# An output product turned around: the stationary and the moving operand of the second MoE's last product change places, and the work beside it is spread differently

## The chip, the core and the metric

The kernel runs on one core of a Trainium2 chip, in one launch. The metric is the device time of that core in microseconds (us), as the median of the runs. A profiled execution gives the trace; its "span" is the time from the first to the last recorded event on the core, and its own run time is a little more than that.

## The reference, cut to what matters

Three parts follow one another: local attention over 4 x 8 heads x 768 positions (with 8 memory keys), a first MoE with a squared ReLU, and a second, gated MoE. All three run over the same 3072 tokens of width 512. The change touches only the end of the third part:

```
def _moe2_ref(x, w_gate, w_val, w_out):      # x: 3072 x 512
    g = x @ w_gate                           # 512 x 1536
    silu = g * (1.0 / (1.0 + np.exp(-g)))
    val = x @ w_val                          # 512 x 1536
    return (silu * val @ w_out)              # 1536 x 512  ->  3072 x 512
```

All is float32. The result is 3072 x 512.

## The kernel before, in words

**Precision.** Every float32 operand of a large product is split into a high part (a cast to fp32r, "hi") and the rest ("lo", the source minus hi). A product is three matmul passes: hi x hi, hi x lo, lo x hi. Making a split costs one cast on ScalarE (ACT, line 96) and one subtraction (line 99), on VectorE (DVE) or GpSimd (POOL), whichever the call names.

**Seven products for eight.** The second MoE treats its operands as 2 x 2 blocks and forms seven block products instead of eight, from sums of blocks. The sums of the weights are prepared earlier and lie in DRAM (`w2d`); the core streams them back four at a time, 1 MB (`load_chunks`, line 515), into five rotating buffers `wst`. The load of a group waits until the group five before it has been used.

**Stages.** The 3072 tokens are worked through in four stages s = 0 to 3 of 768 tokens (two halves of 384, `NT2`). A stage has two parts:

- The *gated* part (line 610), 12 blocks f of 7 products. A product (line 599) is six matmuls: the weight chunk is stationary (128 x 128), z, the stage's transposed input, moves 384 tokens wide. DVE and ACT combine the seven accumulators into two blocks of u = silu * val, which lie in `uf`, with tokens along the free dimension. Its accumulators are the four PSUM banks `abanks`.
- The *output* part (lines 844 to 856), called "b" in the plan: 42 items j, seven groups i of six (`NP`), one group for each block product of u with `w_out`. Here line 656 takes u as the stationary operand, 128 tokens at a time, and moves the weight sum 256 columns wide: three token tiles by three passes, nine matmuls for an item. A group adds up in one of two accumulators of two banks (`pbank`, line 581), used in turn. When a group is done, `combine` (line 681) reads that accumulator: ACT for group 0, DVE for the others (one instruction; two for group 5). The combination of group i is issued after item 6(i+1), and group i+2 may not begin before it has been read. Four of the seven combinations end in an output block of 384 tokens x 256 columns, which `store` (line 674) writes to DRAM from SyncE's queue, after the next item.

In the last stage the last group is taken apart instead: `item_rows` (line 663) forms one 128-token tile at a time over all six items, in a bank of its own, so that the combination (line 867) and the store of one tile run beside the next.

**The ring.** The items read hi and lo of a block of u from a ring of ten slots (`NRING`). Splits 0 to 9 are made in the gated part. The split for item j+10 is issued after item j, because it takes j's slot.

**Order.** All engines run in an order written out by hand; each engine works its own instructions strictly in that order. What runs beside the items is planned at lines 803 to 824: a dictionary from a place ("after item j") to the calls issued there. In the output part the plan holds, besides the 32 splits 10 to 41 (`split_u`; the subtraction on POOL where j % 3 == 2, else on DVE, line 816):

- the last block sums of u on POOL (`sum_u`): S1 and S2 of the last pair after item 0, and six S4, one after each of items 12 to 17 (line 814);
- in stages 0 to 2, the work on the next stage's z (lines 819 to 824): eleven calls at items 0 to 24: two splits of 128 x 768 (ACT cast, DVE subtraction), four block sums on DVE (line 563), and five more splits.

Within one place the order is: the combination, S4, the split of u, the work on z.

Of the kernel before, what the change touches and what calls it, by code (L numbers as in the profile page):

```python
# [7 lines left out]
F32 = mybir.dt.float32  # L8
# [4 lines left out]
ALU = mybir.AluOpType  # L13
# [11 lines left out]
DM, FF1, FF2 = 512, 2048, 1536  # L25
KD = DM // 128
NF1, NF2 = FF1 // 128, FF2 // 128
NTOK = B * S
BLOCKS = (4, 4, 4, 4, 4, 4, 4, 4)
NTM = GQ * max(BLOCKS)  # L30
NT2 = 384
# [13 lines left out]
QC = 2 * 128  # L45
NP = NF2 // 2
GVC, WOC = 7 * NF2, 7 * NP
NCH = GVC + WOC
NRING = 10
# [19 lines left out]
def attention_moe_moe_kernel(ctx, tc, att, v0, w1, w2, out):  # L69
# [8 lines left out]
    nc = tc.nc  # L78
    pe, act, dve, pool, sp = nc.tensor, nc.scalar, nc.vector, nc.gpsimd, nc.sync
# [9 lines left out]
    hbank = [ps.tile([128, 512], F32, name=f"hbank{i}") for i in range(2)]  # L89
    abank, yb0 = (ps.tile([128, 2, 512], F32, name=n) for n in ("abank", "yb0"))  # L90
# [24 lines left out]
    rows = []  # L115
# [195 lines left out]
    for t, n in enumerate(BLOCKS[1:], 1):  # L311
        for j in range(n):
            e = 13 * j + 12 if t == 1 else QB * (t - 1) + (j + 1) * QB // n - 15
# [201 lines left out]
    def load_chunks(g):  # L515
        if 4 * g >= NS * NCH:
            return
        t = chunks[g] = wp.tile([128, 4, 2, QC], R, tag="w", name="wst")
        n = 0
        while n < 4:  # L520
            c = (4 * g + n) % NCH
            m = min(4 - n, NCH - c)
            sp.dma_start(out=t[:, n:n + m].bitcast(F32), in_=w2d[:, c:c + m])
            n += m

    def chunk(n):
        t = chunks[n // 4]
        return [t[:, n % 4, h] for h in range(2)]
# [45 lines left out]
    def double():  # L574
        return up.tile([128, 2 * NT2], F32, tag="tmp", name="tmp", bufs=6)

    uf, ring = [], []
    SLOT = {"A11": 0, "A21": 1, "A12": 2, "A22": 3, "S3": 4, "S1": 1, "S2": 0, "S4": 2}
    ITEMS = ("A11", "A12", "S2", "S3", "A22", "S1", "S4")
    abanks = [*hbank, *yb1]  # L580
    pbank = [b.rearrange("p a c -> p (a c)")[:, 0:2 * NT2] for b in (abank, yb0)]

    def u_of(p, name):
        k = SLOT[name]
# [59 lines left out]
        dve.tensor_tensor(second, c22, u4, ALU.mult)  # L644
        side(6)

    def item(s, j):
        i, p = divmod(j, NP)
        uh, ul = ring[(WOC * s + j) % NRING]
        n = NCH * s + GVC + j  # L650
        whi, wlo = chunk(n)
        to = pbank[(7 * s + i) % 2]
        for t in range(3):
            rows = slice(128 * t, 128 * t + 128)
            for m, (u, wt) in enumerate(((uh, whi), (ul, whi), (uh, wlo))):
                pe.matmul(  # L656
                    to[:, QC * t:QC * t + QC], u[:, rows], wt,
                    start=p == 0 and m == 0 and t != 1, stop=p == NP - 1 and m == 2 and t != 0,
                )
        if n % 4 == 3:  # L660
            load_chunks(n // 4 + 5)

    def item_rows(s, t, to):
        rows = slice(128 * t, 128 * t + 128)
        for p in range(NP):
            j = 6 * NP + p
            uh, ul = ring[(WOC * s + j) % NRING]
            whi, wlo = chunk(NCH * s + GVC + j)
            for m, (u, wt) in enumerate(((uh, whi), (ul, whi), (uh, wlo))):
                pe.matmul(to, u[:, rows], wt, start=p == 0 and m == 0, stop=p == NP - 1 and m == 2)  # L670

    acc, ready = {}, []

    def store(s, h, e, o, t0=0, n=3):
        r0 = (2 * s + h) * NT2 + 128 * t0
        sp.dma_start(
            out=out[r0:r0 + 128 * n, e * QC:(e + 1) * QC].rearrange("(t p) c -> p t c", p=128),
            in_=o.rearrange("p (t c) -> p t c", c=QC),
        )

    def combine(s, i):
        p = pbank[(7 * s + i) % 2]
        if i == 0:
            acc["x"] = double()
            act.copy(acc["x"], p)
        elif i == 2:
            dve.tensor_tensor(acc["x"], p, acc["x"], ALU.add)  # L687
        elif i == 3:
            acc["y"] = double()
            dve.tensor_tensor(acc["y"], p, acc["x"], ALU.add)  # L690
        else:
            o = double()
            if i == 4:
                dve.tensor_tensor(o, acc["y"], p, ALU.subtract)
            else:
                dve.tensor_tensor(o, p, acc["y" if i == 5 else "x"], ALU.add)
            if i == 5:
                dve.tensor_tensor(acc["x"], p, acc["x"], ALU.add)
            h, e = {1: (0, 0), 4: (1, 0), 5: (1, 1), 6: (0, 1)}[i]
            ready.append((s, h, e, o))  # L700
# [19 lines left out]
    for c in range(NC2):  # L720
        a = QB * (P2 + c // 4) + (4, 18, 32, 44)[c % 4]
# [14 lines left out]
    def side(hs):  # L736
# [8 lines left out]
        out=eye, in_=eye, pattern=[[-1, GQ]], base=0, channel_multiplier=1, compare_op=ALU.is_equal, fill=0.0,  # L745
# [54 lines left out]
    def job(key, fn, *args):  # L800
        jobs.setdefault(key, []).append((fn, args))

    for s in range(NS):
        for p in range(NP):
            f = 2 * p + 1
            job((s, f, 0), split_u, s, p, pool)
            job((s, f, 1), sum_u, p, "S3")
            last_pair = p == NP - 1
            key = (s, "b", 0) if last_pair else (s, f + 1, 1)
            job(key, sum_u, p, "S1")  # L810
            job((s, "b", 0) if last_pair else (s, f + 1, 2), sum_u, p, "S2")
            if NP + p < NRING:
                job((s, f + 1, 4), split_u, s, NP + p, pool)
            job((s, "b", 2 * NP + p), sum_u, p, "S4")
        for j in range(NRING, WOC):
            job((s, "b", j - NRING), split_u, s, j, pool if j % 3 == 2 else dve)
        if s + 1 < NS:
            job((s, 6, 3), load_z, s + 1)
            for at_j, fn, *args in (
                (0, split_b1, 0), (2, split_b1, 1), (4, sum_t, "T1"), (6, sum_t, "T3"), (8, sum_t, "T2"),  # L820
                (10, sum_t, "T4"), (12, split_t, "T2"), (15, split_t, "T3"), (18, split_t, "T1"), (21, split_t, "T4"),
                (24, split_t, "B22"),
            ):
                job((s, "b", at_j), fn, s + 1, *args)

# [3 lines left out]
    for tags in (("gh", "gl"),) * 3 + (("r", "r"),):  # L829
        n = 3 if tags[0] == "gh" else 2  # L830
        ring.append([gp.tile([128, NTM], R, tag=tag, name="ring", bufs=n) for tag in tags])
    for _ in range(2):
        t = rawp.tile([128, WC], R, tag="cut", name="ring", bufs=CB)
# [6 lines left out]
    for s in range(NS):  # L840
        for f in range(NF2):
            gated(s, f, lambda slot: work(s, f, slot))
        final = s == NS - 1
        for j in range(WOC - NP * final):
            item(s, j)
            for args in ready:
                store(*args)
            ready.clear()
            if j and j % NP == 0:
                combine(s, j // NP - 1)  # L850
            work(s, "b", j)
        if not final:
            combine(s, 6)
            for args in ready:
                store(*args)
            ready.clear()
    s = NS - 1
    for t in range(3):
        p = abanks[t][:, 0:QC]
        item_rows(s, t, p)  # L860
        if t == 0:
            combine(s, 5)
            for args in ready:
                store(*args)
        cols = slice(QC * t, QC * t + QC)
        o = double()[:, 0:QC]
        dve.tensor_tensor(o, p, acc["x"][:, cols], ALU.add)
        store(s, 0, 1, o, t, 1)
    ordered.close()
    uctx.close()  # L870

# [67 lines left out]
```

## Time and profile before

| | |
|---|---|
| Time, median of 3 runs | 1152.96 us (1150.97 to 1153.2) |
| The profiled execution's own time | 1155.3 us |
| Its span | 1153.6 us, 22369 instructions |
| TensorE (PE) busy | 1137.2 us (99%), 8804 matmuls |
| VectorE (DVE) busy | 719.7 us (62%) |
| ScalarE (ACT) busy | 551.7 us (48%) |
| GpSimd (POOL) busy | 348.1 us (30%) |
| DMA | 245.24 MB, mean 213 GB/s |

"Busy" is the time in which an instruction of that engine was recorded as running. Matmuls are pipelined: one of 384 columns is recorded as 334 ns long, but the next one starts before it has ended. So PE's 99% does not say how many columns a microsecond carries; the step from one matmul to the next is read from the length of a run of matmuls in the chain of waits, divided by their number. A stage of the second MoE lasts about 134 us; the four output parts begin at 703, 837, 971 and 1105 us.

### The profile page before, as it was taken

What the parts mean: (1) busy time and instruction counts of PE and PEld (TensorE: products, weight loads), DVE (VectorE), ACT (ScalarE), POOL (GpSimd) and SP (SyncE); (2) the same over time, 40 slices, a digit from 0 to 9 for tenths busy, and PEclk for the clock granted to TensorE, in tenths of its full rate; (3) what the DMA queues carried; (4) which work ended last, traced back from release to release, by engine and by line L of the source; (5) the groups of instructions that cost most, each with busy time, mean ns of one, the idle gap of its engine ahead of it and who ended that gap; (6) DMA issues with size and microseconds to landing.
All of it is one profiled execution on the core that took longest, in us unless ns stands there. A gap on an engine that the chain in (4) does not pass through costs nothing.

```text
span 1153.6 us, 22369 instructions
## 1 busy us (share of the span) xinstructions
PE 1137.2 (99%) x8804; PEld 1120.9 (97%) x8804; DVE 719.7 (62%) x1216; ACT 551.7 (48%) x1348; POOL 348.1 (30%) x317
## 2 busy tenths in 40 slices
PE   6999999999999999999999999999999999999998
PEld 5999999999999999999999999999999999999998
DVE  6897445656655565563324668766696667956654
ACT  5896546666666667664452224322252223512242
POOL 0000001453425525250001335423371334713353
PEclk9999999999999999999999999999999999999999
DMA  9731204547665476550255866788777787787772
GB/s 376 298 126 53 89 27 152 205 169 254 213 216 193 172 238 245 197 178 9 83 182 236 290 219 214 260 276 293 270 265 262 259 309 252 243 292 254 255 283 98
DMA packets 81897, 245.24 MB, mean 213 GB/s; under 512 B 6272, under 2 KB 52864, under 8 KB 61568
## 3 DMA queue, kind: packets, MB, share of 16 engines
q1 hardware_dynamic: 81792, 243.82, 60.2%
q8 instruction: 69, 1.13, 0.4%
q14 instruction: 36, 0.29, 0.1%
HBM read 198.18 MB, written 45.61 MB: 211 GB/s over the span
## 4 chain that ended last, share of the span: by engine, by line
PE 96%; DVE 2%; DMA 1%; ACT 0%; issue 0%; SPq 0%; ACTq 0%; DVEq 0%
PE hbank L375 24%; PE yb L419 24%; PE hbank L605 15%; PE yb L605 15%; PE abank L656 7%; PE yb L656 6%; PE abank L272 2%; PE abank L150 2%; DVE ring L99 1%; PE hbank L210 1%; DMA first_v<-in_v_dram 1%; PE hbank L670 0%; DVE zraw L563 0%; DVE z L99 0%; DVE w L99 0%
## 5 line engine op out<-in xcount | busy, mean ns | idle before, releaser
L375 PE MATMUL hbank<-x,w 128*128 128x384 f32 (+1 forms) x1548 | 293.9, 338 | 0.0
L375 PEld LDWEIGHTS hbank<-x,w 128*128 128x128 f32 x1548 | 273.7, 191 | 0.8 <-issue 0.2
L400 DVE TENSOR_TENSOR gl<-r,gh 128x384 fp32r<-128x384 f32 x128 | 87.2, 682 | 228.7 <-ACT r L394 228.5
L419 PE MATMUL yb<-gh,w 128*128 128x384 f32 x1024 | 205.0, 337 | 0.0
L419 PEld LDWEIGHTS yb<-gh,w 128*128 128x128 f32 x1024 | 178.7, 188 | 2.2
L99 POOL TENSOR_TENSOR ring<-uf,ring 128x384 fp32r<-128x384 f32 x84 | 97.5, 1164 | 273.7 <-PE hbank L605 141.7
L592 POOL TENSOR_TENSOR uf<-uf 128x384 f32<-128x384 f32 x96 | 109.7, 1159 | 124.0 <-DVE uf L644 124.0
L605 PE MATMUL hbank<-w,wst 128*128 128x384 f32 x720 | 138.3, 334 | 0.0
L605 PE MATMUL yb<-w,wst 128*128 128x384 f32 x720 | 138.3, 334 | 0.0
L474 POOL TENSOR_TENSOR wraw<-cut 128x256 f32<-128x256 f32 x36 | 26.5, 737 | 347.1 <-DVE sm L239 262.8
L383 ACT ACTIVATE r<-hbank 128x384 f32<-128x384 f32 x128 | 63.0, 492 | 133.5 <-PE hbank L375 133.1
L605 PEld LDWEIGHTS hbank<-w,wst 128*128 128x128 f32 x720 | 126.0, 188 | 0.0
L605 PEld LDWEIGHTS yb<-w,wst 128*128 128x128 f32 x720 | 126.0, 188 | 0.0
L96 ACT CAST ring<-uf 128x384 fp32r<-128x384 f32 x168 | 85.9, 511 | 58.2 <-PE yb L656 28.9
L419 PE MATMUL yb<-gl,w 128*128 128x384 f32 x512 | 113.2, 334 | 0.0
L643 ACT ACTIVATE tmp<-tmp 128x384 f32<-128x384 f32 x48 | 25.2, 526 | 173.0 <-DVE tmp L642 173.0
L656 PE MATMUL abank<-wst,ring 128*128 128x256 f32 x756 | 93.1, 283 | 2.3 <-ACT ring L96 2.3
L656 PEld LDWEIGHTS abank<-wst,ring 128*128 128x128 f32 x756 | 91.8, 192 | 2.6 <-ACT ring L96 2.6
L419 PEld LDWEIGHTS yb<-gl,w 128*128 128x128 f32 x512 | 90.9, 188 | 0.0
L656 PE MATMUL yb<-wst,ring 128*128 128x256 f32 x702 | 86.4, 283 | 1.2 <-DVE tmp L687 1.2
L226 ACT ACTIVATE prob<-abank,mx 96x72 f32<-96x72 f32 x224 | 67.6, 310 | 40.6 <-DVE mx L218 40.3
L253 DVE STREAM_TRANSPOSE pT<-prob 32x256 f32<-32x256 f32 x196 | 85.1, 434 | 2.5
(128 smaller groups left out, 1513.6 us busy)
## 6 DMA issues: line engine op xcount, KB each, us to landing
wst<-w2d SPq DMA_DIRECT2D x124, 1024.0 KB, 5.0
wraw<-in_w_dram SPq DMA_DIRECT2D x34, 1024.0 KB, 6.4
qk<-in_att_dram SPq DMA_DIRECT2D x28, 464.0 KB, 5.3
w2d<-wraw SPq DMA_DIRECT2D x48, 256.0 KB, 2.5
v<-in_att_dram SPq DMA_DIRECT2D x28, 256.0 KB, 5.1
y1d<-ys SPq DMA_DIRECT2D x8, 768.0 KB, 4.5
w2d<-wraw SPq DMA_DIRECT2D x12, 512.0 KB, 3.0
zraw<-y1d SPq DMA_DIRECT2D x8, 768.0 KB, 7.9
```

The costliest lines, as they stand in the source:

```text
L96: act.copy(hi, src)
L99: lo_engine.tensor_tensor(lo, src, hi.bitcast(F32), ALU.subtract)
L226: act.activation(probs[u % 2][:, h, 0:WK], s["s"][:, r, i], AF.Exp, bias=s["mx"][:, r, i:i + 1], scale=SCALE, accum_out=s["sm"][:, h],)
L253: dve.transpose(pT[row:row + 32, :, 32 * c:32 * c + 32], probs[u % 2][32 * c:32 * c + 32, :, col:col + 32],)
L375: pe.matmul(hbank[f % 2][:, cols], wt[:, k * 128:(k + 1) * 128], x[:, k, cols], start=i == 0, stop=i == 3 * KD - 1,)
L383: act.activation(r, hbank[f % 2][:, 0:n], AF.Relu)
L400: dve.tensor_tensor(gl, g["r"], g["gh"].bitcast(F32), ALU.subtract)
L419: pe.matmul(ybank[e][:, 0:nt_of[t]], wt[:, c:c + 128], gtile[t, f][g], start=f == 0 and p == 0, stop=f == NF1 - 1 and p == 2,)
L474: pool.tensor_tensor(o, x, y, op)
L592: pool.tensor_tensor(u_of(p, o), u_of(p, x), u_of(p, y), op)
L605: pe.matmul(to, wt[:, k * 128:k * 128 + 128], x[:, k], start=m == 0, stop=m == 5)
L656: pe.matmul(to[:, QC * t:QC * t + QC], u[:, rows], wt, start=p == 0 and m == 0 and t != 1, stop=p == NP - 1 and m == 2 and t != 0,)
```

## The change

1. The output product is turned around. Line 656's matmul now has a 128-column slice of the weight sum as its stationary operand and moves u, 384 tokens wide; an item is two column halves k by three passes. The accumulator is one bank per half (128 output columns x 384 tokens, instead of 128 tokens x 256 columns by three). The output in DRAM becomes 512 x 3072, and is turned back outside the launch.
2. The combinations and the stores take the new layout (128 x 2 x 384 for 128 x 768; pieces of 384 elements in DRAM for pieces of 256).
3. The last group of the last stage is formed in two halves k instead of three token tiles.
4. The plan: S4 of pair p comes after item 5p + 4 (before: 12 + p). The subtraction of split j is on POOL where j % 4 == 1 (before: j % 3 == 2). The eleven calls on the next z stand after items 0, 3, 6, 9, 12, 15, 18, 22, 26, 30, 34 (before: 0, 2, 4, 6, 8, 10, 12, 15, 18, 21, 24), in the same order.

```diff
-    pbank = [b.rearrange("p a c -> p (a c)")[:, 0:2 * NT2] for b in (abank, yb0)]
+    pbank = [b[:, :, 0:NT2] for b in (abank, yb0)]
...
-    def item(s, j):
+    def item_pe(s, j, k, to):
         i, p = divmod(j, NP)
         uh, ul = ring[(WOC * s + j) % NRING]
+        whi, wlo = chunk(NCH * s + GVC + j)
+        for m, (u, wt) in enumerate(((uh, whi), (ul, whi), (uh, wlo))):
+            pe.matmul(
+                to[k], wt[:, 128 * k:128 * k + 128], u, start=p == 0 and m == 0, stop=p == NP - 1 and m == 2,
+            )
+
+    def item(s, j):
         n = NCH * s + GVC + j
-        whi, wlo = chunk(n)
-        to = pbank[(7 * s + i) % 2]
-        for t in range(3):
-            rows = slice(128 * t, 128 * t + 128)
-            for m, (u, wt) in enumerate(((uh, whi), (ul, whi), (uh, wlo))):
-                pe.matmul(
-                    to[:, QC * t:QC * t + QC], u[:, rows], wt,
-                    start=p == 0 and m == 0 and t != 1, stop=p == NP - 1 and m == 2 and t != 0,
-                )
+        to = pbank[(7 * s + j // NP) % 2]
+        for k in range(2):
+            item_pe(s, j, k, [to[:, 0], to[:, 1]])
...
-    def store(s, h, e, o, t0=0, n=3):
-        r0 = (2 * s + h) * NT2 + 128 * t0
+    def store(s, h, e, o, k0=0):
+        t0 = (2 * s + h) * NT2
+        n = o.shape[1]
+        r0 = e * QC + 128 * k0
         sp.dma_start(
-            out=out[r0:r0 + 128 * n, e * QC:(e + 1) * QC].rearrange("(t p) c -> p t c", p=128),
-            in_=o.rearrange("p (t c) -> p t c", c=QC),
+            out=out[r0:r0 + 128 * n, t0:t0 + NT2].rearrange("(k p) t -> p k t", p=128), in_=o,
         )
...
-            job((s, "b", 2 * NP + p), sum_u, p, "S4")
+            job((s, "b", 5 * p + 4), sum_u, p, "S4")
         for j in range(NRING, WOC):
-            job((s, "b", j - NRING), split_u, s, j, pool if j % 3 == 2 else dve)
+            job((s, "b", j - NRING), split_u, s, j, pool if j % 4 == 1 else dve)
...
-                (0, split_b1, 0), (2, split_b1, 1), (4, sum_t, "T1"), (6, sum_t, "T3"), (8, sum_t, "T2"),
-                (10, sum_t, "T4"), (12, split_t, "T2"), (15, split_t, "T3"), (18, split_t, "T1"), (21, split_t, "T4"),
-                (24, split_t, "B22"),
+                (0, split_b1, 0), (3, split_b1, 1), (6, sum_t, "T1"), (9, sum_t, "T3"), (12, sum_t, "T2"),
+                (15, sum_t, "T4"), (18, split_t, "T2"), (22, split_t, "T3"), (26, split_t, "T1"), (30, split_t, "T4"),
+                (34, split_t, "B22"),
...
     s = NS - 1
-    for t in range(3):
-        p = abanks[t][:, 0:QC]
-        item_rows(s, t, p)
-        if t == 0:
+    for k in range(2):
+        to = hbank[k][:, 0:NT2].rearrange("p (k n) -> p k n", k=1)
+        for p in range(NP):
+            item_pe(s, 6 * NP + p, k, [to[:, 0]] * 2)
+        if k == 0:
             combine(s, 5)
             for args in ready:
                 store(*args)
-        cols = slice(QC * t, QC * t + QC)
-        o = double()[:, 0:QC]
-        dve.tensor_tensor(o, p, acc["x"][:, cols], ALU.add)
-        store(s, 0, 1, o, t, 1)
+        o = double_k()[:, 0:1]
+        dve.tensor_tensor(o, to, acc["x"][:, k:k + 1], ALU.add)
+        store(s, 0, 1, o, k)
```

`double_k()` is `double()` (line 574) seen as 128 x 2 x 384.

## Rows read from the trace of the kernel before

**Rows 1.** The page, part 1 (busy time) and part 4 (chain's shares by engine):
```profile
PE 1137.2 (99%) x8804; PEld 1120.9 (97%) x8804; DVE 719.7 (62%) x1216; ACT 551.7 (48%) x1348; POOL 348.1 (30%) x317
PE 96%; DVE 2%; DMA 1%; ACT 0%; issue 0%; SPq 0%; ACTq 0%; DVEq 0%
```

**Rows 2.** The chain of waits over the span: start us, length us, work xmatmuls:
```profile
615.57 2.08 PE hbank L605 x12
...
702.93 6.47 PE abank L656 x54
...
722.36 6.49 PE yb L656 x54
729.95 6.71 PE abank L656 x54
...
749.62 2.08 PE hbank L605 x12
...
883.76 2.08 PE hbank L605 x12
...
971.13 6.47 PE abank L656 x54
...
1017.86 2.08 PE hbank L605 x12
...
1105.23 6.47 PE yb L656 x54
...
1144.10 4.32 PE hbank L670 x36
1148.41 2.17 PE yb L670 x18
```

**Rows 3.** Groups of PE instructions, whole span: count | busy us, mean ns | idle before:
```profile
L656 PE MATMUL abank<-wst,ring 128*128 128x256 f32 x756 | 93.1, 283 | 2.3 <-ACT ring L96 2.3
L656 PE MATMUL yb<-wst,ring 128*128 128x256 f32 x702 | 86.4, 283 | 1.2 <-DVE tmp L687 1.2
```

**Rows 4.** PE's timeline where stage 1's output part begins: start us, length us:
```profile
836.83 0.87 PE L656 MATMUL yb<-wst,ring 128*128 128x256 f32 x6
```

**Rows 5.** Who waited for whom, PE, 610 to 1154 us: total, times, longest:
```profile
PE abank L656 <- ACT ring L96: 2.3, 2, 1.2
PE yb L656 <- DVE tmp L687: 1.2, 1, 1.2
```

**Rows 6.** DVE's timeline in stage 0's output part: start us, length us, operation:
```profile
703.07 0.55 DVE L642 TENSOR_TENSOR tmp<-yb,tmp 128x384 f32<-128x384 f32 x1
...
704.75 0.55 DVE L99 TENSOR_TENSOR ring<-uf,ring 128x384 fp32r<-128x384 f32 x1
...
709.91 1.37 DVE L99 TENSOR_TENSOR ring<-uf,ring 128x384 fp32r<-128x384 f32 x1
711.20 0.95 DVE L563 TENSOR_TENSOR zraw<-zraw 128x768 f32<-128x768 f32 x1
...
721.65 1.77 DVE L99 TENSOR_TENSOR w<-tmp,w 128x768 fp32r<-128x768 f32 x1
...
725.92 1.77 DVE L99 TENSOR_TENSOR w<-zraw,w 128x768 fp32r<-128x768 f32 x1
...
728.90 0.94 DVE L687 TENSOR_TENSOR tmp<-abank,tmp 128x768 f32<-128x768 f32 x1
```

**Rows 7.** POOL's timeline in the same stretch:
```profile
721.24 4.35 POOL L592 TENSOR_TENSOR uf<-uf 128x384 f32<-128x384 f32 x3
...
739.51 1.01 POOL L99 TENSOR_TENSOR ring<-uf,ring 128x384 fp32r<-128x384 f32 x1 [2.20 <-ACT ring L96]
```

**Rows 8.** Stage 0's output part: length, busy of PE, PEld, DVE, ACT, POOL; clock, DMA:
```profile
702.77:749.62 46.85, 45.74 (x380) 45.56 (x380) 39.23 (x41) 21.89 (x41) 26.58 (x19) 1.00 0.75 250
```

**Rows 9.** The end, all engines' timeline:
```profile
1150.61 0.42 DVE L867 TENSOR_TENSOR tmp<-yb,tmp 128x256 f32<-128x256 f32 x1 [1.73 <-PE yb L670]
```

**Rows 10.** DMA issues from 1135 us to the end: count, KB each, median us to landing:
```profile
out_dram<-tmp SPq DMA_DIRECT2D x2, 384.0 KB, 2.6
out_dram<-tmp SPq DMA_DIRECT2D x3, 128.0 KB, 1.7
```

More of the change, by code (lines that the diff above doesn't have):

```diff
@@ L645, in gated, with double_k @@
         side(6)
-    def item(s, j):
+    def item_pe(s, j, k, to):
         i, p = divmod(j, NP)
         uh, ul = ring[(WOC * s + j) % NRING]
-        n = NCH * s + GVC + j
-        whi, wlo = chunk(n)
-        to = pbank[(7 * s + i) % 2]
-        for t in range(3):
-            rows = slice(128 * t, 128 * t + 128)
-            for m, (u, wt) in enumerate(((uh, whi), (ul, whi), (uh, wlo))):
-                pe.matmul(
-                    to[:, QC * t:QC * t + QC], u[:, rows], wt,
-                    start=p == 0 and m == 0 and t != 1, stop=p == NP - 1 and m == 2 and t != 0,
-                )
+        whi, wlo = chunk(NCH * s + GVC + j)
[4 more added lines that the diff above has]
+    def item(s, j):
+        n = NCH * s + GVC + j
+        to = pbank[(7 * s + j // NP) % 2]
+        for k in range(2):
+            item_pe(s, j, k, [to[:, 0], to[:, 1]])
         if n % 4 == 3:
             load_chunks(n // 4 + 5)
[L663 to L670, printed above, removed]
-    acc, ready = {}, []
-    def store(s, h, e, o, t0=0, n=3):
-        r0 = (2 * s + h) * NT2 + 128 * t0
+    acc, ready = {}, []
+    def double_k():
+        return double().rearrange("p (k n) -> p k n", k=2)
+    def store(s, h, e, o, k0=0):
+        t0 = (2 * s + h) * NT2
+        n = o.shape[1]
+        r0 = e * QC + 128 * k0
         sp.dma_start(
-            out=out[r0:r0 + 128 * n, e * QC:(e + 1) * QC].rearrange("(t p) c -> p t c", p=128),
-            in_=o.rearrange("p (t c) -> p t c", c=QC),
+            out=out[r0:r0 + 128 * n, t0:t0 + NT2].rearrange("(k p) t -> p k t", p=128), in_=o,
         )
@@ L683, in combine @@
         if i == 0:
-            acc["x"] = double()
+            acc["x"] = double_k()
             act.copy(acc["x"], p)
@@ L688, in combine @@
         elif i == 3:
-            acc["y"] = double()
+            acc["y"] = double_k()
             dve.tensor_tensor(acc["y"], p, acc["x"], ALU.add)
         else:
-            o = double()
+            o = double_k()
             if i == 4:
@@ L933 @@
         args.append(nc.dram_tensor(f"in_{name}_dram", a.shape, _mybir.dt.from_np(a.dtype), kind="ExternalInput").ap())
-    args.append(nc.dram_tensor("out_0_dram", (NTOK, DM), F32, kind="ExternalOutput").ap())
+    args.append(nc.dram_tensor("out_0_dram", (DM, NTOK), F32, kind="ExternalOutput").ap())
     with _tile.TileContext(nc) as tc:
@@ L937 @@
     r = _run(nc, [arrays], core_ids=[0])
-    return r.results[0]["out_0_dram"]
+    return _np.ascontiguousarray(r.results[0]["out_0_dram"].T)
```

## The prediction

> **What bounds the kernel now.** I read the page first. PE is busy 99% of the span and makes up 96% of the chain that ended last [rows 1]; no other engine carries more than 2% of it. So the time moves when PE's stream gets shorter or when PE stops waiting inside it, and hardly otherwise. Busy time doesn't tell how long the stream is, because matmuls overlap. For that I went to the chain of waits, which prints runs of matmuls with a start and a length [rows 2]. Two steps come out of it:
>
> - the 384-wide matmuls with a weight chunk stationary (line 605): 2.08 us for 12, that is 173.3 ns from one to the next;
> - the 256-wide matmuls of the output part (line 656): 6.48 us for the 54 of a group (6.47 and 6.49 are printed), that is 120.0 ns.
>
> The stage table gives a granted clock of 1.00 in the output part [rows 8], full speed, 2.4 GHz: 384 columns are 160.0 ns there and 256 are 106.7 ns. Both steps stand 13.3 ns above their columns. A matmul thus costs its columns plus the same 13.3 ns here, whatever its width.
>
> Second, the waits inside the stream. An output part of 42 items without a wait lasts 7 x 6.48 = 45.36 us. From the starts in the chain [rows 2], stage 0 takes 749.62 - 702.93 = 46.69 us, stage 2 takes 1017.86 - 971.13 = 46.73. For stage 1 the chain leaves PE at the start, so I take it from PE's timeline, which shows matmuls 0.16 us ahead of the chain's reckoning (702.77 opens the stretch of rows 8, 702.93 the chain's run): 836.83 + 0.16 = 836.99 [rows 4], so 883.76 - 836.99 = 46.77. Lost: 1.33 + 1.41 + 1.37 = 4.11 us. Stage 3, which has no next z to prepare, takes 1144.10 - 1105.23 = 38.87 for six groups, 6 x 6.48 = 38.88: nothing lost.
>
> Where is it lost? In stage 0 the fourth group ends at 722.36 + 6.49 = 728.85 and the fifth begins at 729.95, 1.10 us late, and then runs 0.23 us longer (6.71). The table of waits has one such wait per stage, 2.3 and 1.2 us in all, two of them put down to ACT's cast into the ring and one to DVE's line 687 [rows 5]. The first name misleads. Group 4 uses the accumulator of group 2, and line 687 is what empties it; DVE ran it at 728.90 for 0.94 us [rows 6], just up to the late start, although group 2 had ended at 722.36. DVE was some 6.5 us behind. So PE waits once per z stage for DVE's backlog.
>
> **The change part by part.** *The matmuls.* An item goes from 9 x 120.0 = 1080 ns to 6 matmuls of 384. The columns stay the same (2304); three matmuls go, with 3 x 13.3 = 40 ns. The trace of before has no item of the new form. From both sides: line 605 with the same width and the same kind of stationary tile (`wst`) gives 173.3 ns, 1040 ns an item; if the step of line 656 grew with its columns, it would be 180.0 ns and nothing would be gained. I take 173.3, as the nearest row in width, operand and clock. Count: line 656 has 756 + 702 = 1458 matmuls [rows 3], line 670 has 36 + 18 [rows 2]: 1512, or 168 items. 1512 x 120.0 = 181.4 us become 1008 x 173.3 = 174.7: **-6.7 us** (0 to -6.7).
>
> The Trainium skill ("TensorE: Matmul & The Clock Gate", section "Back-to-back issue gap") gives N / 2.4 + 2.5 ns for a warm matmul, and by that rule turning the product around is worth next to nothing: 3 x 2.5 = 7.5 ns an item, an estimated 1.3 us in all. The rows don't follow it: both widths stand 13.3 ns above their columns, not 2.5. It is a rival below for the case that the new form comes nearer to it.
>
> *The wait for DVE.* Line 687 of group 2 is issued after item 18; group 4 begins with item 24. Items get shorter, so PE is there earlier: 24 x 1.040 = 24.96 us after the start of the part, instead of 25.92. What stands ahead of line 687 on DVE, from the plan:
>
> - before: the subtractions of splits 10 to 27 less the six on POOL, 12; four z subtractions (places 0, 2, 12, 15); four z sums; one combination;
> - after: 14 subtractions (four on POOL); two z subtractions (0, 3; the others are at 18 and later, behind line 687); four sums; one combination.
>
> DVE's operations on two SBUF operands come in two lengths: 0.55 or 1.37 us for 384 columns, 0.95 or 1.77 for 768 [rows 6]. The difference, 0.82 us, is the same at both, and it goes with POOL running: POOL's own operation takes 4.35 / 3 = 1.45 us beside DVE and 1.01 alone [rows 7]. So a POOL operation costs DVE up to 0.82 us. POOL has 14 ahead of that point before (S1, S2, six splits, six S4) and 9 after (S1, S2, four splits, S4 of items 4, 9, 14). The sum for DVE, from its start on this queue 1.82 us into the part (704.75 - 702.93):
>
> - before: 12 x 0.55 + 4 x 0.95 + 4 x 0.95 + 0.95 = 15.2; 14 x 0.82 = 11.5; with 0.94 for line 687 itself and 1.82: 29.4 us. Measured: 729.84 - 702.93 = 26.9. The sum is 2.5 too high, since not every POOL operation meets one of DVE's.
> - after: 14 x 0.55 + 2 x 0.95 + 4 x 0.95 + 0.95 = 14.4; 9 x 0.82 = 7.4; with 0.94 and 1.82: 24.5 us at most.
>
> 24.5 is before 24.96 even with every meeting counted; with the surplus of the sum before taken off in proportion (2.5 x 9 / 14 = 1.6) it is 22.9, and the accumulator is free 2 us early. The wait is gone: **-4.1 us** over three stages. From both sides: if all that DVE gained were the two z subtractions (2 x 1.77) less two more splits at their worst (2 x 1.37), line 687 would end 0.8 us earlier, with PE 0.96 earlier too: the late start would be 1.10 + 0.96 - 0.80 = 1.26, with the 0.23 after it 1.49 a stage, 4.5 in all, 0.4 more than now. Below nothing isn't to be had.
>
> *What is late next.* The second half gets what the first half loses. A POOL operation cost DVE (11.5 - 2.5) / 14 = 0.64 us on average before; I use that from 22.9 us on. Line 690 (group 3) has to end before item 30, at 31.2 us: ahead of it stand four subtractions of u, two of z and three POOL operations, with its own 0.94 together 6.9 us, so it ends near 29.8. Line 694 (group 4) has to end before item 36, at 37.4: five of u, one of z, three of POOL and 0.94 are 6.5, so near 36.3. Both hold, with 1.1 to 1.4 us in hand. The last z split is issued after item 34 (36.4 us); its result (B22) is first read by the seventh product of the next gated part, 43.7 + 6 x 1.04 = 49.9 us after the start. The splits of u have a lead of nine items (9.4 us), and DVE is at most some 4 us behind (22.9 less 18.7, where item 18 begins). POOL's 19 operations become 16; S4 of pair 5 comes after item 29, its split after item 31, ten items before item 41. Nothing of POOL is late.
>
> *What costs nothing.* Combinations read the same 768 columns. SyncE's queue holds the stores ahead of chunk loads, and a store waits for its combination; DVE comes earlier, so the loads behind it aren't later. Chunks are needed every 4.16 us instead of 4.32, the pace of the gated part (4 x 6 x 173.3 ns), in which PE waited for nothing [rows 5]. All of this is hidden by PE's stream; the bare price would show as PE waiting for `wst`.
>
> *The end.* The last group is in the 168 items. Behind the last matmul stands one DVE operation of 384 columns, 0.55 [rows 6], for one of 256, 0.42 [rows 9]; and a store of 192 KB for 128 KB. 384 KB landed in 2.6 us and 128 in 1.7 [rows 10], so 192 is near 1.9: **+0.35 us** (0 to +1.0).
>
> *Sum.* -6.7 - 4.1 + 0.35 = -10.5 us. The profiled execution (span 1153.6, 1155.3 in all, 1.7 outside) would become a span of 1143.1 and 1144.8; it lies 2.3 above the median of the runs. Against the median: 1152.96 - 10.5 = **1142.5 us**. Where no item waits, z stages' output parts last 42 x 1.040 = 43.7 us.
>
> **The rivals.**
>
> 1. *The wait stays, or moves to a later group.* PE arrives 0.96 us earlier and DVE gains no more than that, or line 690 or 694 is late in place of line 687. For it: the lower bound above, and margins of only 1 us in the second half. Against it: five POOL operations fewer ahead of line 687. Then 1152.96 - 6.7 + 0.4 + 0.35 = 1147.0; half of it, 1144.8.
> 2. *The new form saves less.* By columns alone, 180.0 ns a matmul, it saves nothing: 1152.96 - 4.1 + 0.35 = 1149.2. Against it: line 605's 173.3 ns at that width. By the Trainium skill's rule above, 2.5 ns for each of 504 matmuls fewer, it would be an estimated 1147.9.
> 3. *Slower: DVE becomes the bound of the z stages.* It now has 24 of the 32 subtractions of u instead of 21. If each of its 35 operations on two SBUF operands met POOL: 24 x 1.37 + 11 x 1.77 + 7 x 0.94 = 58.9 us against 43.7. Its last z result is read 6.2 us into the next part, so the output part would last about 58.9 - 6.2 = 52.7 us, 6 longer than now, and the kernel 1152.96 + 3 x 6 - 1.3 (stage 3 and the end) = 1169.7. It begins to decide when DVE takes more than 43.7 + 6.2 = 49.9 us. Against it: POOL has only 16 operations, at most 16 x 0.82 = 13.1 us of meetings on 24 x 0.55 + 11 x 0.95 + 7 x 0.94 = 30.2, that is 43.3; DVE is busy 39.2 us in the same stretch now [rows 8].
>
> **How the numbers follow.** The forecast has 0.78 (1141 to 1144.2: the runs shown spread by 1 us either side, and the end is open by some tenths); the wait that stays in whole or half or moves, 0.13 (1144.8 to 1147); the new form saving less, 0.05; slower by DVE, 0.02; the rest is for what I don't see. The range 1140.8 to 1147.0 holds the first two cases. 0.2%, 2.3 us, is about what a measurement of this kernel can tell from no change: faster by more 0.95, within 0.03, slower 0.02.
>
> **What would show it.** In the profile after, the items' matmuls run in the chain at 6.24 us for 36, 173.3 ns each; 6.48 us for 36 would be by columns. The three z stages' output parts last 43.7 us and the stage-3 one 6 x 6.24 = 37.4; line 687's combination of group 2 ends before item 24, and PE's table of waits has no entry in them. If it still has one at the fifth group, the step on DVE's queue is wrong; if it has one at another group, the step on the second half is. A new wait for `wst` or a part beyond 47 us would make the whole wrong.

## The result

| | before | after |
|---|---|---|
| Time, median | 1152.93 us (1150.97 to 1153.2, 4 runs) | 1142.83 us (1140.31 to 1143.89, 4 runs) |
| Ratio to before | | 0.9913, 95% interval 0.9893 to 0.9932 |
| Span of the profiled execution | 1153.6 us | 1141.0 us |
| Matmuls | 8804 | 8300 |

Forecast was 1142.5 us. The page after, its busy times and its chain by engine:

```profile
PE 1128.5 (99%) x8300; PEld 1112.5 (98%) x8300; DVE 717.4 (63%) x1227; ACT 551.8 (48%) x1348; POOL 328.1 (29%) x305
PE 98%; DMA 1%; SPq 0%; DVE 0%; ACT 0%; issue 0%; ACTq 0%
```

DVE's 2% of the chain [rows 1] is gone, and PE's table of waits has no entry between 600 us and the end. The chain of waits after (start us, length us, work; the items are line 652 now):

```profile
700.85 6.24 PE abank L652 x36
707.09 6.24 PE yb L652 x36
713.33 6.24 PE abank L652 x36
719.57 6.24 PE yb L652 x36
725.81 6.24 PE abank L652 x36
732.05 6.24 PE yb L652 x36
738.29 6.24 PE abank L652 x36
...
831.89 6.24 PE yb L652 x36
...
869.33 6.24 PE yb L652 x36
...
962.93 6.24 PE abank L652 x36
...
1000.37 6.24 PE abank L652 x36
...
1093.97 6.24 PE yb L652 x36
...
1125.17 6.24 PE abank L652 x36
1131.41 6.26 PE hbank L652 x36
```

Each group begins where the one before it ends. The output part of stage 0 takes 744.53 - 700.85 = 43.68 us, and so do those of stages 1 and 2 (875.57 - 831.89, 1006.61 - 962.93), for 46.69, 46.77 and 46.73 before [rows 2, 4]. A matmul takes 6.24 / 36 = 173.3 ns.

DVE's timeline in stage 0, its line for group 2's combination being 683 now, then those for groups 3 and 4:

```profile
722.70 0.94 DVE L683 TENSOR_TENSOR tmp<-abank,tmp 128x768 f32<-128x768 f32 x1
...
727.17 0.94 DVE L686 TENSOR_TENSOR tmp<-yb,tmp 128x768 f32<-128x768 f32 x1
...
733.72 0.94 DVE L690 TENSOR_TENSOR tmp<-tmp,abank 128x768 f32<-128x768 f32 x1
```

Group 2's ends at 723.64, 22.8 us into the part (26.9 before [rows 6]); item 24 begins at 725.81. The stage's row (length, busy of PE, PEld, DVE, ACT, POOL, clock, DMA), against [rows 8]:

```profile
700.69:744.53 43.84, 43.84 (x254) 43.84 (x254) 37.51 (x44) 22.01 (x41) 21.28 (x16) 1.00 0.78 270
```

DVE executes three operations more than before and is busy 1.7 us less, beside three operations fewer on POOL (e6 to e8 below bear on that).

The two profiled spans differ by 12.6 us, not by 10.5. From the start of stage 0's output part to the last matmul's end (702.93 to 1150.58 before, 700.85 to 1137.67 after) the kernel lost 10.83 us: 6.72 + 4.11 as summed up. The end grew from 3.02 to 3.33. The other 2.08 us were gone before stage 0's output part began, in code that is the same in both: 0.69 us had been gained when a run of 40 matmuls near 32 us began, right after the opening's loads, and 1.42 us in this run (0.03 came back behind it), whose length differs between executions. In the chains of before, after, and e1 below:

```profile
31.92 10.39 PE hbank L375 x40
```
```profile
31.23 8.97 PE hbank L375 x40
```
```profile
30.96 7.03 PE hbank L375 x40
```

That is 260, 224 and 176 ns a matmul of 288 columns, where 120.0 ns of columns and 13.3 would be 133 (an estimate from the two steps of the prediction). The table of stretches gives the granted clock as 1.00 over this run, in before too (third number from the end):

```profile
31.92:42.31 10.39, 10.39 (x41) 10.39 (x42) 6.68 (x11) 6.15 (x23) 0.00 (x0) 1.00 1.02 418
```

So the trace does not show what holds PE there, and the cause stays open. The run took 6.67 to 10.39 us in the eleven profiles that have it whole. The two shortest belong to e1 and e5, in executions some 3 us faster than the median of their kernels, so this run may be most of the 3 us by which runs of one kernel differ; an execution without a trace can't show it.

### The profile page after: what moved, and what is told of

The parts are those of the page before. It is cut to its first block, busy times and chain, and to the rows that moved or that the text cites. A ratio compares the mean times of both kernels' runs of the same rounds, so it can differ in the third digit from the quotient of the medians.

```text
span 1141.0 us, 21345 instructions
## 1 busy us (share of the span) xinstructions
PE 1128.5 (99%) x8300; PEld 1112.5 (98%) x8300; DVE 717.4 (63%) x1227; ACT 551.8 (48%) x1348; POOL 328.1 (29%) x305
## 4 chain that ended last, share of the span: by engine, by line
PE 98%; DMA 1%; SPq 0%; DVE 0%; ACT 0%; issue 0%; ACTq 0%
PE hbank L375 24%; PE yb L419 24%; PE yb L605 15%; PE hbank L605 15%; PE abank L652 8%; PE yb L652 7%; PE abank L272 2%; PE abank L150 2%; PE hbank L210 1%; DMA first_v<-in_v_dram 1%; PE hbank L652 1%; PE yb L192 0%; SPq L125 0%; DVE x L287 0%; DVE tmp L863 0%
## 5 line engine op out<-in xcount | busy, mean ns | idle before, releaser
L99 POOL TENSOR_TENSOR ring<-uf,ring 128x384 fp32r<-128x384 f32 x72 | 81.1, 1126 | 283.5 <-ACT ring L96 143.7
L592 POOL TENSOR_TENSOR uf<-uf 128x384 f32<-128x384 f32 x96 | 106.1, 1116 | 123.6 <-DVE uf L644 123.6
L652 PE MATMUL abank<-ring,wst 128*128 128x384 f32 x504 | 89.6, 334 | 0.0
L652 PEld LDWEIGHTS abank<-ring,wst 128*128 128x128 f32 x504 | 87.6, 188 | 0.0
L652 PE MATMUL yb<-ring,wst 128*128 128x384 f32 x468 | 83.2, 334 | 0.0
```

Of the source, the lines that this page charges most:

```text
L99: lo_engine.tensor_tensor(lo, src, hi.bitcast(F32), ALU.subtract)
L592: pool.tensor_tensor(u_of(p, o), u_of(p, x), u_of(p, y), op)
L652: pe.matmul(to[k], wt[:, 128 * k:128 * k + 128], u, start=p == 0 and m == 0, stop=p == NP - 1 and m == 2,)
```

## The experiments

Theory: the turned product saves 40 ns an item, and DVE's backlog, which the plan removes, keeps an accumulator occupied. Rivals: the wait was for ACT's cast into the ring; or the new product, not the plan, removed it; or another law for the step of a matmul.

**e1: the product alone**, with the old plan.

```diff
-            job((s, "b", 5 * p + 4), sum_u, p, "S4")
+            job((s, "b", 2 * NP + p), sum_u, p, "S4")
-            ... pool if j % 4 == 1 else dve)      # z at 0, 3, 6, ... 34
+            ... pool if j % 3 == 2 else dve)      # z at 0, 2, 4, ... 24
```

> The product turned around (384 wide, six matmuls an item), with the old plan for the next z, S4 and the subtractions. Theory (DVE's backlog holds the accumulator, and only the plan removes that): group 2's combination ends 26 to 27 us after the start of a z stage's output part, as before, while item 24 could now begin at 24.96; so PE waits once per z stage, at the fifth group, 1.5 to 2.2 us, longer than the 1.1 us before, with 0.2 us after it. Output parts of the z stages 45.4 to 46.1 us, stage 3 without a wait; 1142.8 + 3 x 2.1 = about 1149. Rival (the new layout of the accumulators, one bank per column half, by itself lets DVE empty them in time): no wait, output parts 43.7 us, 1142.8.

1154.63 us (1151.21 to 1155.29, 10 runs), ratio to before 1.001 (0.9997 to 1.0024): the turned product alone gains nothing, and the time is 5.6 us above the theory's forecast. The chain gives the output parts as 46.8, 48.4 and 46.8 us, 10.9 us of waits and their sequels in all. Three things are in its rows.

```profile
717.93 6.52 PE yb L652 x36
726.46 6.48 PE abank L652 x36
...
860.63 8.07 PE yb L652 x36
```

DVE's rows for the accumulators of groups 1 and 2:

```profile
716.84 0.94 DVE L692 TENSOR_TENSOR tmp<-yb,tmp 128x768 f32<-128x768 f32 x1
...
725.41 0.94 DVE L683 TENSOR_TENSOR tmp<-abank,tmp 128x768 f32<-128x768 f32 x1
```

First, group 3 starts late too (717.93 for 717.36): it needs group 1's accumulator, and line 692 empties that only at 717.78. I had looked at group 4 only. Second, group 4 begins 2.02 us after group 3's end and 2.86 us after the place that it could have had (698.64 + 24.96 = 723.60), where 1.5 to 2.2 were expected: group 2's combination ends at 726.35, 27.7 us into the part, and not 26 to 27. Group 3's late start adds nothing to this, because group 4 waits for that combination in any case. The group behind each wait takes 0.24 to 0.28 us more; with group 4's 0.24 a stage loses 3.1 us. Third, in stage 1 group 4 takes 8.07 us for 6.24. The stage table of that stretch (columns as above; the third from the end is the granted clock):

```profile
860.00:862.00 2.00, 1.36 (x8) 1.40 (x9) 2.00 (x4) 0.05 (x1) 0.47 (x1) 1.00 0.29 119
862.00:864.00 2.00, 2.00 (x8) 2.00 (x7) 2.00 (x4) 1.58 (x3) 0.00 (x0) 0.52 0.00 0
864.00:866.00 2.00, 2.00 (x9) 2.00 (x9) 2.00 (x4) 0.54 (x2) 1.01 (x1) 0.62 0.68 164
866.00:868.00 2.00, 2.00 (x13) 2.00 (x12) 1.53 (x3) 0.92 (x3) 0.00 (x0) 1.00 0.85 360
```

After a wait of 2.13 us the granted clock fell to half and stayed there over most of 4 us: another 1.6 us. In this profile the waits of about 2.0 us in stages 0 and 2 had no such sequel. Of the waits of before, none over 1.2 us, none had one. Averaged over the span, the granted clock was 0.997 to 0.999 in the ten runs of e1 and 1.000 in the fifteen of before. That fits such falls in more than the one profile, but the runs without a trace do not show where the clock was lower.

**e2: the plan alone**, with the old product.

> The old product (256 wide, nine matmuls an item) with the new plan for the next z, S4 and the subtractions. Theory: the wait goes with the plan alone, each output part is 42 x 1.080 = 45.36 us, and the kernel gains 4.1 us: 1148.8. Rival (the wait went because of the new product): the wait of 1.1 + 0.23 us stays in each z stage, 1152.9.

1149.25 us (1146.83 to 1150.03, 6 runs), ratio 0.9957 (0.9943 to 0.9972). Every group takes 6.48 us and follows the one before; PE's table of waits has no entry in these parts. The fourth and fifth groups of stage 0 in the chain:

```profile
720.74 6.48 PE yb L656 x54
727.22 6.48 PE abank L656 x54
```

As the theory has it, the plan removes the wait by itself. Together with e1: the plan alone is worth 3.9 us, the product alone -1.5 (before beside them: 1153.13), both 10.1 (before beside it: 1152.93). The two parts are not independent.

**e4 and e4b: a third accumulator** under the old plan, so that DVE may stay late.

> As e1_product_only (new product, old plan), but the groups use three accumulators in turn instead of two (the third one in the two banks that the gated part leaves free); the last group of the last stage goes to the two other free banks. Theory (PE waits for DVE to empty the accumulator of group 2, not for ACT's cast into the ring): the fifth group now needs the accumulator of group 1, long empty, and the wait goes though DVE is as late as in e1 (group 2's combination still ends 25 to 27 us into the part): output parts 43.7 us, 1142.8. Rival (the wait is one for ACT's cast into the ring, as the table of waits calls it): the wait at the fifth group stays, 1149.

1247.69 us (4 runs), ratio 1.0814 (1.0792 to 1.0835). I had made one tile of the two banks `hbank`, and in the gated part PE now waited wherever DVE or ACT still read the other bank of that tile. The largest of seven such entries (line 606 is the product, 636 a sum):

```profile
PE hboth L606 <- DVE tmp L636: 13.4, 12, 1.1
```

The gated part of stage 1 grew from 87.4 to about 109 us. So the total says nothing on the question; the output parts took 43.7 us without a wait. e4b repeats it with the banks as two tiles:

```diff
+        i = j // NP
+        to = [b[:, 0:NT2] for b in hbank] if i % 3 == 2 else [pbank[i % 3][:, 0], pbank[i % 3][:, 1]]
...                                          # combinations of groups 2 and 5: one instruction for each bank
-        to = hbank[k][:, 0:NT2].rearrange("p (k n) -> p k n", k=1)
+        to = yb1[k][:, 0:NT2].rearrange("p (k n) -> p k n", k=1)
```

> New product, old plan, three accumulators in turn as in e4_third_accumulator, but the third one stays two separate one-bank tiles (hbank), so that the gated part is untouched; the combinations of groups 2 and 5 are two instructions of 384 columns each instead of one of 768. Theory (PE waits for DVE to empty an accumulator, and nothing else in these parts is late): every wait of e1 goes, output parts 43.7 us in all stages, 1142.8, though the plan is the old one and the combination of group 2 still ends 25 us or more after the start. Rival (DVE's lateness also holds the ring or SyncE's queue of chunk loads, so that it costs in any case): waits stay, at later items, and the time lies between 1146 and 1155.

1143.17 us (1140.26 to 1143.63, 4 runs), ratio 0.9911 (0.9894 to 0.9927), the changed kernel's time with the old plan. The chain, then DVE's row for group 2:

```profile
720.28 6.24 PE abank L652 x36
726.52 6.24 PE yb L652 x36
```
```profile
728.33 1.01 DVE L687 TENSOR_TENSOR tmp<-hbank,tmp 128x384 f32<-128x384 f32 x2
```

DVE is as late as in e1 (729.34, 27.8 us into the part), and the fifth group starts at 726.52 all the same. So in e1 PE waited for an occupied accumulator and for nothing else in these parts. The two entries that named ACT's cast [rows 5] were the same wait under another name.

**e5, e6, e7: one part of the plan back**, in the changed kernel.

> The changed kernel with only the work on the next z at its old places (0 to 24). Ahead of group 2's combination stand 14 subtractions of u, four of z, four sums, one combination and nine POOL operations at 0.64 to 0.82 us: it ends 24.8 to 26.4 us into the part, against 24.96 for item 24. Theory: a wait of 0 to 1.4 us at the fifth group in each z stage, without the fall of the clock that came after 2.0 us: 1143 to 1148, about 1146. Rival (the places of z carry the whole gain of the plan): as e1, 1154.6. Rival (z is not what made DVE late): 1142.8.

> The changed kernel with only the six S4 back at items 12 to 17. DVE's own work ahead of group 2's combination is that of the changed kernel, but 12 POOL operations instead of 9 stand beside it: 24.8 to 27.0 us at 0.64 to 0.82 us each, against 24.96. Theory (POOL's operations on two SBUF operands hold DVE's up): a wait of 0 to 2 us at the fifth group of the z stages, 1143 to 1149, about 1145.5. Rival (POOL's sums don't matter to DVE): 1142.8.

> The changed kernel with only the old choice of POOL's subtractions (j % 3 == 2: 11 of 32, instead of 8). Ahead of group 2's combination: 12 subtractions of u on DVE instead of 14, 11 POOL operations instead of 9: 23.1 to 25.1 us against 24.96. Theory: two subtractions fewer on DVE (1.1 us) are outweighed by two more meetings with POOL (1.3 to 1.6), but the margin holds in most groups: 1142.8 to 1144. Rival (giving DVE more subtractions made it later, so that the old choice leaves more room): 1142.8 with the combination of group 2 ending earlier than in the changed kernel (723.64 - 700.85 = 22.8 us).

| put back | median us (range) | ratio to before (95%) | z stages' output parts, us | late groups |
|---|---|---|---|---|
| e5: places of z | 1145.15 (1142.52 to 1146.41) | 0.993 (0.9913 to 0.9947) | 44.41, 44.49, 44.48 | 3 and 4 |
| e6: S4 | 1143.93 (1141.47 to 1144.2) | 0.9918 (0.9903 to 0.9932) | 44.01, 44.03, 44.02 | 4 |
| e7: choice of POOL's subtractions | 1144.9 (1144.37 to 1145.42) | 0.993 (0.9914 to 0.9947) | 44.17, 44.12, 44.16 | 5 |

The intervals of all three overlap the changed kernel's, so the run times alone do not part them from it; the traces do. The groups are counted from 0. In the traces e5 loses 2.3 us, e6 1.0 and e7 1.4 over three stages of 43.68 us. No part carries the plan: put back alone, the three cost 4.8 us together; put back at once (e1), 10.9. e5's expectation named group 4 alone; group 3, which needs group 1's accumulator, is late there before it, as in e1.

e6 is the plainest test of POOL's share: DVE has the same operations ahead of group 2's combination as in the changed kernel, and POOL three more beside them. DVE's row for it, and group 4 in the chain:

```profile
724.96 0.94 DVE L683 TENSOR_TENSOR tmp<-abank,tmp 128x768 f32<-128x768 f32 x1
```
```profile
726.01 6.51 PE abank L652 x36
```

It ends at 725.90, 24.9 us into the part (700.99), 2.1 later than in the changed kernel, or 0.7 us for each POOL operation. Group 4 could have begun at 725.95 and is 0.06 late, with 0.27 behind it; PE's table of waits lists no wait as short as that, so the starts in the chain are the surer test. In e7 group 5 is the late one; it waits for the combination of group 3 (line 686):

```profile
PE yb L652 <- DVE tmp L686: 0.5, 2, 0.3
```
```profile
725.09 0.94 DVE L683 TENSOR_TENSOR tmp<-abank,tmp 128x768 f32<-128x768 f32 x1
```

The combination of group 2 there (second row) ends at 726.03, 24.3 us into the part, 1.5 later than in the changed kernel, although DVE has two operations fewer ahead of it. Two more operations on POOL outweigh them, as the theory had it; the expectation that the margin would hold in most groups was too good, and the median lies 0.9 us above its range.

**e8: no subtraction on POOL.**

```diff
-            job((s, "b", j - NRING), split_u, s, j, pool if j % 4 == 1 else dve)
+            job((s, "b", j - NRING), split_u, s, j, dve)
```

> The changed kernel with all 32 subtractions of the output part on DVE, none on POOL, which keeps only its eight sums (S1, S2, six S4). Ahead of group 2's combination: 18 subtractions of u on DVE (0.55 each), 5 POOL operations: 18 x 0.55 + 2 x 0.95 + 4 x 0.95 + 0.95 + 0.94 + 1.82 = 19.3, with 5 x 0.64 to 0.82 22.5 to 23.4 us, as in the changed kernel (22.8), against 24.96. Theory (a subtraction given to POOL costs DVE about as much as doing it): no wait, 1142.8, though DVE has a third more of them. Rival (DVE's count of operations sets when it is late): ten operations more than before, waits at the fifth group, 1146 to 1154.

1144.12 us (1143.37 to 1144.97), ratio 0.993 (0.9908 to 0.9951), whose interval overlaps the changed kernel's; output parts 43.8 us, no entry in PE's waits. Group 2's combination ends at 725.60, 23.8 us into the part, 0.4 above the upper end of the sum. DVE's row for it, and the stage's row over a stretch as long as the changed kernel's:

```profile
724.66 0.94 DVE L683 TENSOR_TENSOR tmp<-abank,tmp 128x768 f32<-128x768 f32 x1
```
```profile
701.60:745.44 43.84, 43.84 (x254) 43.70 (x254) 37.70 (x52) 22.02 (x41) 11.03 (x8) 1.00 0.77 268
```

Taking eight operations from POOL halves its time (21.28 to 11.03) and costs DVE 0.2 us (37.51 to 37.70), not 8 x 0.55 = 4.4.

**e3 and e3b: narrower matmuls**, same columns.

```diff
+            for c in (0, 192):                       # e3b: (0, 128, 256), 128 wide
                 pe.matmul(
-                    to[k], wt[:, 128 * k:128 * k + 128], u, ...
+                    to[k][:, c:c + 192], wt[:, 128 * k:128 * k + 128], u[:, c:c + 192], ...
```

> The changed kernel with each output matmul cut into two of 192 tokens: same operands, same columns, twice as many matmuls. Theory (a matmul costs its columns at full clock plus 13.3 ns, whatever its width and whatever its operands): 192 / 2.4 + 13.3 = 93.3 ns, 6.72 us for a group of 72, +80 ns for each of 168 items: 1142.8 + 13.4 = 1156.2. Rival (not the width but the exchange of operands made the items shorter; with weights stationary only columns count): 6.24 us a group, 1142.8. By the Trainium skill's figure (TensorE: Matmul & The Clock Gate, Back-to-back issue gap) of 2.5 ns for each further matmul it would be 1008 x 2.5 = 2.5 us more, an estimated 1145.3.

> The changed kernel with each output matmul cut into three of 128 tokens. At 192 tokens one took 8.04 us / 72 = 111.7 ns, not 93.3. Theory now (below some 236 columns the weight load of the next matmul sets the pace, 111.7 ns for 128 stationary columns, whatever moves): 108 x 111.7 = 12.06 us a group, 6 matmuls of 3 parts by 111.7 less 1040 is 0.97 us an item more, 1142.8 + 168 x 0.97 = about 1306. Rival (narrower matmuls cost a larger constant, 111.7 - 80 = 31.7 ns beside their columns): 53.3 + 31.7 = 85.0 ns, 9.18 us a group, 1142.8 + 168 x 0.49 = 1225.

e3: 1192.32 us (1190.59 to 1193.67), ratio 1.0336 (1.0316 to 1.0356); e3b: 1305.5 us (one run). A group in each chain:

```profile
709.37 8.04 PE yb L653 x72
```
```profile
712.67 12.06 PE yb L653 x108
```

Both are 111.7 ns a matmul, for 192 columns as for 128. e3's expectation missed by 36 us: columns and 13.3 ns hold at 256 and 384, but there is a floor of 111.7 ns at 192 and 128. e3b, expected from that floor at 1306, met it. The Trainium skill ("TensorE: Matmul & The Clock Gate", section "LDWEIGHTS (loading the stationary operand)") gives P / 1.2 ns for a weight load of P columns, 106.7 for 128. The measured floor lies 5 ns above that, and the profile's pages count as many loads (PEld) as matmuls (PE), so the load may be what sets it; a load's recorded length, 192 ns in e3 and e3b, does not tell its step. No run here left loads out or made them narrower, so that the load is the cause is not shown.

## Why the prediction was right

- *The matmuls, -6.7 us.* 173.3 ns after, as line 605 showed; 168 items by 40 ns is 6.72. The step that was too wide is "whatever its width": the law holds at 256 and 384 columns, and e3 breaks it at 192. The prediction used it only at the two widths where it holds. The Trainium skill's rule of 2.5 ns a matmul ("TensorE: Matmul & The Clock Gate", section "Back-to-back issue gap"), which would have left an estimated 1.3 us, does not fit the 120.0 and 173.3 ns here; that section gives it for an isolated matmul and says that in a stream of loads and matmuls both set the spacing.
- *The wait, -4.1 us.* All three went. The sum on DVE's queue put group 2's combination at 22.9 us (24.5 at most); it ended at 22.8, in all three stages. That it fits to 0.1 us is partly luck, since sums of the same kind missed by 2.5 us in the second half and by 0.4 in e8. e4b shows the mechanism, e2 that the plan does it alone, and e6 that POOL's operations are part of DVE's lateness.
- *The second half.* Expected ends 29.8 and 36.3 us (groups 3 and 4); measured 27.3 and 33.8, so the sum was 2.5 us on the safe side there. e7 shows that the margin is real but small: two POOL operations more and group 5 is late.
- *The end.* +0.31 us for +0.35: DVE 0.56 us for 384 columns, and 192 KB landed in 1.9 us.

```profile
out_dram<-tmp SPq DMA_DIRECT2D x2, 192.0 KB, 1.9
```

- *The step that was too kind:* the price of the first rival. "The wait stays" was put at no more than 1.49 us a stage and 1147.0 us. That bound let DVE gain 0.8 us; under the plan of before it gains none, and the same sum would give 2.29 (1.10 + 0.96 + 0.23). There the new product really pays 3.1 to 4.7 us a stage and stands at 1154.6 (e1). Missing were 0.8 us by which group 2's combination comes later in the part than before (27.7 for 26.9), which make up the 3.1, and in one stage the fall of the clock after a wait of 2.13 us. Why DVE came later there is not shown. The sum of the two terms was right because both are in the change; each alone is worth less than its term or nothing.

## What to carry to other kernels

Where one engine's stream bounds the kernel and its matmuls are already dense, the step from one matmul to the next (length of a run in the chain, divided by its count) shows whether a wider moving operand pays: three matmuls fewer saved 40 ns of 1080, and narrower matmuls cost dearly once the step no longer falls with the width (111.7 ns at 192 and at 128 columns). Shortening the bound engine's work pulls every deadline of the others forward: check each buffer that is handed back, not only the one that was late. Giving work to a second engine gains little when each operation there delays the first by about as much as it saves: here some 0.6 to 0.7 us (at most 0.8) against an operation of 0.55.

## What the runs showed of the hardware beyond that

- One matmul with its own 128-column weight load took 111.7 ns at 128 and 192 moving columns (e3b, e3), 120.0 at 256 (before), 173.3 at 384 (after), at a granted clock of 1.00.
- A wait of 2.13 us in a dense stream was followed by the granted clock at half for most of 4 us, behind one of the three waits of 2.0 us or more in that profile (e1).
- The recorded length of a matmul does not show these steps: 334 ns for 384 columns (173.3 apart), 283 for 256 [rows 3] (120.0 apart), 274 and 275 for 192 and 128 (111.7 apart).
- One POOL operation more on two SBUF operands made DVE 0.7 us later on average (e6), and eight subtractions moved from POOL to DVE made DVE only 0.2 us busier (e8).
